# Attention into a mixture block on one core: q and k prepared for four heads at once, scores as three 64-row products, v loaded twice

## The chip, the cores and the metric

The kernel runs on one core of a Trainium2 chip. The metric is device time in microseconds (us), lower is better. Runs of the same kernel agree within about 0.3%.

The core has a matrix engine (TensorE, PE in the profile; its weight loads are PEld), three elementwise engines (VectorE, DVE; ScalarE, ACT; GpSimd, POOL), a queue engine (SyncE, SP), and 16 DMA engines that all queues share. On-chip memory has 128 partitions (rows). Matrix products land in PSUM, which here is used as banks of 128 x 512 float32.

## The reference

```python
q_n, k_n = rmsnorm(q, g_q), rmsnorm(k, g_k)        # q, k, v: 8 batches, 12 heads, 448 positions, 64 wide
scores = q_n @ k_n.T / sqrt(64)                    # per head, 448 x 448
attn = softmax(scores)                             # the sum gets 1e-9 added
x = (attn @ v), heads side by side                 # 8 x 448 x 768
xk = mu_k * x + (1 - mu_k) * x_prev                # x_prev: x one position earlier
xr = mu_r * x + (1 - mu_r) * x_prev
k = max(xk @ w_k, 0); v = k * k @ w_v              # 768 -> 1024 -> 768
out = sigmoid(xr @ w_r) * v
```

Everything is float32. The kernel multiplies in float16 and carries precision by splitting each operand into a rounded part ("hi") and the rest ("lo"); a product is then hi by hi, hi by lo and lo by hi.

## The kernel before, in words

**Three streams.** `attention()` (line 286) goes through 48 head pairs, six per batch. `weights()` (403) splits the weight matrices in 20 column tiles. `moe(b)` (418) does the three matrix products of a batch and writes the output. All three are Python generators. The loop at 551 takes one step at a time from the stream with the smallest planned time: an attention step advances its clock by 1/`ATT_STEPS` of a batch, so that `moe(b)` is written some 0.2 to 0.25 batches after the attention of batch b. The Tile framework then fixes each engine's order of instructions when the kernel is built, from this written order as priority and from when each instruction could be ready; `QK_PRIORITY` moves the score matmuls 400 places ahead. On the chip each engine follows its fixed order and waits on semaphores.

**One head pair.** Positions are spread so that position 7r + t of a head lies in row r, block t. A pair goes through these steps:

- `load` (139): q, k and v of two heads, each as 128 rows (head, r) of 7 x 64 columns, issued on ScalarE's queue, three or four pairs before that pair's scores.
- `stats` (148): squares of v (155) and of q and k (156) on ScalarE; POOL adds the halves of the squares (159) and multiplies k by the gains (160); VectorE sums (161, 162), scales (163 to 165), and takes 15 reciprocal roots at once by three Newton steps (`rsqrt`, lines 67 to 72). All these small numbers live in tile `ss`.
- `natural` (170): POOL multiplies q and k by their reciprocal norms (180), ScalarE rounds to `hi` (184), POOL subtracts (185), VectorE copies (186) so that `nat` holds 21 blocks of 64 rows x 128, hi and lo next to each other. Two DMA transposes on SyncE (189) make `stk`: for each head, 64 columns of hi stacked on 64 of lo, 128 rows. Then v: scale (191 to 193), hi (195), lo (196), a wrap-around copy (197), and four DMAs on SyncE (201, 202) that copy it on chip into `vv`, once as it is and once shifted by one block on the other 64 rows.
- `group_scores` (220) for groups of two, two, two and one block tiles: a tile of 128 x 448 scores is two matmuls over all 128 rows (234), four half-width ones for the seventh tile, which has one block of each head. Then the row maximum (237, DVE) and the exponential in place (238, ACT). A tile occupies one of four PSUM banks `sc`; in the first six pairs every third takes one of the two `mm` banks.
- `group_probs` (242): reciprocal of the sums (248, 249), hi of the probabilities (254, ACT), lo (255, DVE). Line 255 is the last reader of the bank, which is then free. DMA transposes on SyncE (257, 261) put the probabilities in `pT`.
- `attend` (266): 22 matmuls (273) in eleven passes, two heads each, half the array's columns per head; one pass has 64 rows only.

**Order of a pair's steps.** `attention()` runs the scores of group g + 1 before the probabilities of group g, and spreads `natural` of the next pair and `stats` of the one after over the four groups.

Of the kernel before, what the change touches and what calls it, by code (L numbers as in the profile page):

```python
# [7 lines left out]
F32 = mybir.dt.float32  # L8
# [16 lines left out]
QB = 2 * NT  # L25
# [9 lines left out]
ATT_STEPS = 132  # L35
# [23 lines left out]
def blocks(tile_, off, step):  # L59
    ap = tile_[:, :, :]  # L60
    return bass.AP(tensor=ap.tensor, offset=ap.offset + off, ap=[list(ap.ap[0]), [step, 2], [2 * HD, NT], [1, HD]])
# [13 lines left out]
def attn_moe_kernel(tc, q, k, v, g_q, g_k, mu_k, mu_r, w_k, w_v, w_r, out):  # L75
# [61 lines left out]
    LD, NAT, SUMS, PT, SC = {}, {}, {}, {}, {}  # L137

    def load(i):
        b, hp = pairs[i]  # L140
        pool, n = (pro[0], 1) if i < NP and i % 3 == 2 else (ap_, 2)
        qk = pool.tile([P, 2, S], F32, name="qk", bufs=n)
        vf = pool.tile([P, S], F32, name="vf", bufs=n)
        for dst, src in ((qk[:, 0, :], k), (qk[:, 1, :], q), (vf, v)):
            nc.scalar.dma_start(out=dst, in_=src[b, 2 * hp:2 * hp + 2].rearrange("h (p t) d -> (h p) (t d)", t=NT))
        LD[i] = qk, vf

    def stats(i):
        qk, vf = LD[i]
        qkv = qk.rearrange("p a (t d) -> p (a t) d", d=HD)  # L150
        xs = (pro[0] if i < NP else ap_).tile([P, 2 * NT, HD], F32, name="xn", bufs=1)
        ss = small.tile([P, 48], F32, name="ss", bufs=4)
        ST[i] = ss
        pt = ps.tile([P, 512], F32, name="tr", bufs=1)
        nc.scalar.activation(out=pt[:, 0:S], in_=vf, func=AF.Square, accum_out=ss[:, 45:46])
        nc.scalar.activation(out=xs, in_=qkv, func=AF.Square)
        nc.tensor.matmul(out=pt[:, 0:P], lhsT=ss[:, 45:46].bitcast(BF16)[:, 1:2].broadcast_to([P, P]), rhs=ident16, start=True, stop=True)
        yield
        nc.gpsimd.tensor_tensor(out=xs[:, :, 0:HD // 2], in0=xs[:, :, 0:HD // 2], in1=xs[:, :, HD // 2:], op=ALU.add)
        nc.gpsimd.tensor_tensor(out=qkv[:, 0:NT, :], in0=qkv[:, 0:NT, :], in1=bcast(G[:, :], NT), op=ALU.mult)  # L160
        nc.vector.tensor_reduce(out=ss[:, 0:14], in_=xs[:, :, 0:HD // 2], axis=AX.X, op=ALU.add)
        nc.vector.tensor_reduce(out=ss[:, 14:15], in_=pt[:, 0:P], axis=AX.X, op=ALU.max)
        nc.vector.tensor_scalar(out=ss[:, 7:14], in0=ss[:, 7:14], scalar1=gm[:, 3:4], scalar2=gm[:, 4:5], op0=ALU.mult, op1=ALU.add)
        nc.vector.tensor_scalar(out=ss[:, 0:7], in0=ss[:, 0:7], scalar1=1.0 / HD, scalar2=1e-6, op0=ALU.mult, op1=ALU.add)
        nc.vector.tensor_scalar(out=ss[:, 14:15], in0=ss[:, 14:15], scalar1=TINY, scalar2=2.0 ** -28, op0=ALU.max, op1=ALU.mult)
        yield
        rsqrt(nc, small, ss[:, 16:31], ss[:, 0:15], 15, "rs15")
        yield

    def natural(i):  # L170
# [4 lines left out]
        qk, vf = LD.pop(i)  # L175
        ss = ST.pop(i)
        qkv = qk.rearrange("p a (t d) -> p (a t) d", d=HD)
        sv = ss[:, 30:31]
        xn = ap_.tile([P, 2 * NT, HD], F32, name="xn", bufs=1)
        nc.gpsimd.tensor_tensor(out=xn, in0=qkv, in1=spread(ss[:, 16:30], HD), op=ALU.mult)  # L180
        nat = (pro[0] if i < NP and i % 2 else ap_).tile([P, 3 * NT, 2 * HD], F16, name="nat", bufs=1)
        hi, lo = blocks(nat, 0, QB * 2 * HD), blocks(nat, NT * 2 * HD, NT * 2 * HD + HD)
        xn4 = xn.rearrange("p (a t) d -> p a t d", a=2)
        nc.scalar.copy(out=hi, in_=xn4)  # L184
        nc.gpsimd.tensor_tensor(out=lo, in0=xn4, in1=hi, op=ALU.subtract)  # L185
        nc.vector.tensor_copy(out=nat[:, 0:QB, HD:], in_=nat[:, 0:QB, 0:HD])
        stk = ap_.tile([P, 2, 3 * NT, HD], F16, name="stk", bufs=2)
        for h in range(2):
            nc.sync.dma_start_transpose(out=stk[:, h], in_=nat[h * HD:(h + 1) * HD].rearrange("p a c -> p (a c)"))
        yield  # L190
        nc.vector.tensor_copy(out=st[:, hp:hp + 1], in_=sv)
        nc.vector.tensor_tensor(out=st[:, NP + hp:NP + hp + 1], in0=ss[:, 14:15], in1=sv, op=ALU.mult)  # L192
        nc.vector.tensor_scalar(out=ss[:, 46:47], in0=st[:, NP + hp:NP + hp + 1], scalar1=2.0 ** -15, scalar2=0.0, op0=ALU.mult, op1=ALU.add)
        vw = ap_.tile([P, 2, S + HD], F16, name="vw", bufs=1)
        nc.scalar.activation(out=vw[:, 0, 0:S], in_=vf, func=AF.Copy, scale=sv)
        nc.vector.scalar_tensor_tensor(out=vw[:, 1, 0:S], in0=vf, scalar=sv, in1=vw[:, 0, 0:S], op0=ALU.mult, op1=ALU.subtract)
        nc.vector.tensor_copy(out=vw[:, :, S:], in_=vw[:, :, 0:HD])
        vv = ap_.tile([P, 2, 2, S], F16, name="vv", bufs=2)
        for h in range(2):
            src = vw[h * HD:(h + 1) * HD]  # L200
            nc.sync.dma_start(out=vv[0:HD, h], in_=src[:, :, 0:S])
            nc.sync.dma_start(out=vv[HD:P, h], in_=src[:, :, HD:])
        NAT[i] = stk, vv, ss
        if hp == NP - 1:
            batch_scales(b)
        yield

    def batch_scales(b):
# [4 lines left out]
        nc.vector.tensor_scalar(out=sc[:, 2:4], in0=ismu, scalar1=sc[:, 0:1], scalar2=None, op0=ALU.mult)  # L213
# [6 lines left out]
    def group_scores(i, t0, n):  # L220
        stk, vv, ss = NAT[i]
# [3 lines left out]
        for t in range(t0, t0 + n):  # L225
            if i < PRO and (i * NT + t) % 3 == 2:
                sp = ps.tile([P, 512], F32, name="mm", bufs=MM_BUFS)
            else:
                sp = ps.tile([P, 512], F32, name="sc", bufs=4)
            for j in range(2):  # L230
                for h in (0, 1) if t == NT - 1 else (t % 2,):
                    q0, m, rows = (QB + t, 1, slice(h * HD, (h + 1) * HD)) if t == NT - 1 else (QB + t - h, 2, slice(0, P))
                    with tc.high_priority(offset=QK_PRIORITY):
                        nc.tensor.matmul(  # L234
                        out=sp[rows, 0:S], lhsT=stk[:, h, q0:q0 + m].rearrange("p t c -> p (t c)"),
                        rhs=stk[:, h, j * NT:(j + 1) * NT], start=(j == 0), stop=(j == 1))
# [29 lines left out]
    def attend(i):  # L266
        vv, ss = NAT[i][1:]
# [12 lines left out]
        nc.gpsimd.memset(x[:, 0, 0:1], 0.0)  # L280
        nc.gpsimd.tensor_copy(out=x[:, 0, 1:HD], in_=x[:, NT, 0:HD - 1])
        XT[pairs[i]] = x
        del NAT[i], SUMS[i]
        yield

    def attention():
        groups = [(i, t0, n) for i in range(len(pairs)) for t0, n in ((0, 2), (2, 2), (4, 2), (6, 1))]
        N = len(pairs)
        for i in range(3):
            load(i)  # L290
# [291 lines left out]
```

## Time and profile before

| What | Value |
|---|---|
| Time, median of three runs | 1256.08 us (1255.46 to 1259.13) |
| Span of the profiled execution, first to last instruction (its own time is not given otherwise) | 1253.7 us |
| PE, busy | 994.0 us |
| PEld, busy | 487.8 us |
| DVE, busy | 1019.3 us |
| ACT, busy | 776.9 us |
| POOL, busy | 700.0 us |
| DMA, mean | 155 GB/s |
| Mean granted TensorE clock | 0.929 |

How to read the profile: a row of the groups of instructions gives line, engine, operation, output<-inputs, shapes, count, then busy time in us, mean ns of one, and the idle time just before them with what ended it. A row of the busy times by stretch gives start:end, length, then busy us and count for each engine, the granted clock (1.00 is full), the DMA engines' mean busy share, and GB/s. A row of the timeline gives start in us, duration, engine, line, operation, tiles and shape, and how many were merged; a matmul's duration includes its way through the array, so the distance between starts is its price. A row of the waits reads: engine, line, who released it, us in total, times, longest.

### The profile page before, as it was taken

To read this page: it belongs to the slowest core of one execution; us is meant where nothing else is said; L and a number is where in the kernel's file an instruction comes from. 1 tells how busy PE (TensorE), PEld (TensorE's weight loads), DVE (VectorE), ACT (ScalarE), POOL (GpSimd) and SP (SyncE) were. 2 spreads that over 40 slices of the span, in tenths; PEclk is the share of its full clock that TensorE was granted. 3 is DMA by queue.
4 is the path that set the end of the run, shared out by engine and by line. 5 is a ranking of instruction groups with operands and counts; after the bars stand their busy time and mean duration, and the time that the engine had idled before them with its cause. 6 is when DMAs were issued, how large, how long until landed. Compare 5 with 4: busy or idle time off the path is not lost. (4 is left out here: it accounts for less than half of the span.)

```text
span 1253.7 us, 18496 instructions
## 1 busy us (share of the span) xinstructions
PE 994.0 (79%) x5551; PEld 487.8 (39%) x5551; DVE 1019.3 (81%) x2620; ACT 776.9 (62%) x1756; POOL 700.0 (56%) x702
## 2 busy tenths in 40 slices
PE   1344553766889888898988988989989989889998
PEld 0112221333444344344443444434434444445554
DVE  7989998889989897989778987998898979875200
ACT  3575655566667766677667766767667667755411
POOL 3614665545657664577457554865486557641821
PEclk9986666786999999998999999998999999999999
DMA  5899899889699899888997899988979999968001
GB/s 153 187 214 198 155 182 179 136 186 162 132 183 170 141 178 171 161 169 152 174 192 127 170 166 189 170 159 165 180 148 162 174 186 186 131 111 150 14 13 38
DMA packets 513188, 194.78 MB, mean 155 GB/s; under 512 B 449600, under 2 KB 509504, under 8 KB 513088
## 3 DMA queue, kind: packets, MB, share of 16 engines
q1 hardware_dynamic: 473248, 143.26, 68.2%
q10 hardware_dynamic: 39840, 50.35, 14.8%
q8 instruction: 43, 0.70, 0.2%
q14 instruction: 57, 0.47, 0.1%
HBM read 50.40 MB, written 11.01 MB: 49 GB/s over the span
## 5 line engine op out<-in xcount | busy, mean ns | idle before, releaser
L238 ACT ACTIVATE sc<-sc,sums 128x448 f32<-128x448 f32 x322 | 195.7, 608 | 127.3 <-DVE sums L237 125.5
L234 PE MATMUL sc<-stk 128*128 128x448 f16 (+1 forms) x736 | 191.1, 388 | 99.4 <-DVE ph L255 57.7
L255 DVE SCALAR_TENSOR_TENSOR ph<-sc,sums,ph 128x448 f16<-128x448 f32 x322 | 213.4, 675 | 56.0 <-ACT ph L254 55.6
L254 ACT ACTIVATE ph<-sc,sums 128x448 f16<-128x448 f32 x322 | 188.5, 636 | 93.3 <-DMA pT<-ph 51.3
L428 PE MATMUL mm<-wvh,kk 128*128 128x384 f16 x896 | 236.3, 332 | 4.2 <-DVE th L487 3.4
L428 PE MATMUL mm<-xk,wkh 128*128 128x448 f16 x768 | 220.1, 365 | 18.5 <-ACT kf L450 9.4
L237 DVE TENSOR_REDUCE sums<-sc 128x1 f32<-128x448 f32 x322 | 193.6, 613 | 14.1 <-PE sc L234 13.6
L273 PE MATMUL av<-pT,vv 128*64 128x448 f16 (+1 forms) x1056 | 164.3, 385 | 48.7 <-DMA pT<-ph 32.6
L428 PE MATMUL mm<-wrh,xr 128*128 128x384 f16 x672 | 179.8, 331 | 7.5 <-ACT th L484 2.9
L428 PEld LDWEIGHTS <-kk 128*128 128x128 f16 x1344 | 130.7, 99 | 102.7 <-issue 19.9
L428 PE MATMUL mm<-wvl,kk 128*128 128x384 f16 x448 | 148.4, 331 | 0.0
L428 PE MATMUL mm<-xk,wkl 128*128 128x448 f16 x384 | 139.6, 364 | 0.0
L180 POOL TENSOR_TENSOR xn<-qk,ss 128x896 f32<-128x896 f32 x48 | 82.1, 1711 | 98.0 <-DVE ss L72 50.0
L234 PEld LDWEIGHTS <-stk 128*128 128x128 f16 (+1 forms) x768 | 61.9, 106 | 187.7 <-issue 106.3
L428 PEld LDWEIGHTS <-xr 128*128 128x128 f16 x1008 | 97.2, 99 | 88.1 <-issue 23.5
L185 POOL TENSOR_TENSOR nat<-xn,nat 128x896 f16<-128x896 f32 x48 | 94.6, 1971 | 50.3 <-ACT nat L184 49.1
L273 PEld LDWEIGHTS <-vv 128*64 128x64 f16 (+1 forms) x1056 | 62.4, 114 | 149.4 <-issue 120.5
L428 PEld LDWEIGHTS <-wkh 128*128 128x128 f16 x768 | 75.7, 100 | 98.4 <-issue 33.2
L428 PE MATMUL mm<-wrl,xr 128*128 128x384 f16 x336 | 111.2, 331 | 0.0
L488 POOL TENSOR_TENSOR o<-th,bsc 128x384 f32<-128x384 f32 x48 | 43.4, 904 | 103.3 <-DVE th L487 52.3
L345 DVE SCALAR_TENSOR_TENSOR df<-x,bsc,df 128x448 f32<-128x448 f32 x90 | 83.1, 928 | 18.4 <-POOL df L344 18.3
L452 POOL TENSOR_TENSOR kf<-kf 128x448 f32<-128x448 f32 x64 | 62.9, 983 | 51.0 <-ACT kk L451 51.0
(124 smaller groups left out, 1743.0 us busy)
## 6 DMA issues: line engine op xcount, KB each, us to landing
vv<-vw SPq DMA_DIRECT2D x192, 112.0 KB, 3.3
qk<-in_k_dram ACTq DMA_DIRECT2D x48, 224.0 KB, 3.3
qk<-in_q_dram ACTq DMA_DIRECT2D x48, 224.0 KB, 4.1
vf<-in_v_dram ACTq DMA_DIRECT2D x48, 224.0 KB, 3.3
out_dram<-o SPq DMA_DIRECT2D x56, 192.0 KB, 3.5
raw<-in_moe_w_k_dram ACTq DMA_DIRECT2D x16, 384.0 KB, 4.7
raw<-in_moe_w_v_dram ACTq DMA_DIRECT2D x12, 512.0 KB, 4.0
raw<-in_moe_w_r_dram ACTq DMA_DIRECT2D x12, 384.0 KB, 4.9
```

Of the source, the lines that this page charges most:

```text
L180: nc.gpsimd.tensor_tensor(out=xn, in0=qkv, in1=spread(ss[:, 16:30], HD), op=ALU.mult)
L185: nc.gpsimd.tensor_tensor(out=lo, in0=xn4, in1=hi, op=ALU.subtract)
L234: nc.tensor.matmul(out=sp[rows, 0:S], lhsT=stk[:, h, q0:q0 + m].rearrange("p t c -> p (t c)"), rhs=stk[:, h, j * NT:(j + 1) * NT], start=( ...
L237: nc.vector.tensor_reduce(out=sums[:, t:t + 1], in_=sp[:, 0:S], axis=AX.X, op=ALU.max, negate=True)
L238: nc.scalar.activation(out=sp[:, 0:S], in_=sp[:, 0:S], func=AF.Exp, bias=sums[:, t:t + 1], accum_out=sums[:, 8 + t:9 + t])
L254: nc.scalar.activation(out=ph[:, j, 0:S], in_=sp[:, 0:S], func=AF.Copy, scale=r[:, j:j + 1])
L255: nc.vector.scalar_tensor_tensor(out=ph[:, j, S:], in0=sp[:, 0:S], scalar=r[:, j:j + 1], in1=ph[:, j, 0:S], op0=ALU.mult, op1=ALU.subtract)
L273: nc.tensor.matmul(out=av[h * HD:(h + 1) * HD, 0:S], lhsT=vv[0:kk, h, hl, slot * HD:(slot + 1) * HD], rhs=pT[0:kk, h, c, :], start=(j == 0 ...
L345: nc.vector.scalar_tensor_tensor(out=df, in0=xc, scalar=sc[:, MX + j:MX + j + 1], in1=df, op0=ALU.mult, op1=ALU.add)
L428: nc.tensor.matmul(out=ps_, lhsT=la(i, a), rhs=ra(i, c), start=(i == 0 and a + c == 0), stop=(i == n - 1 and a == 1))
L452: nc.gpsimd.tensor_tensor(out=kf, in0=kf, in1=kf, op=ALU.mult)
L488: nc.gpsimd.tensor_tensor(out=o[:, hs].rearrange("p (c n) -> p c n", n=P), in0=th.rearrange("p (c n) -> p c n", n=P), in1=spread(rsu[:, ND ...
```

## The change

- **Quads.** q and k are prepared for four heads (two pairs) at once by `prep(u)`: tiles of 128 rows (two halves of two heads) x 896, loaded by four DMAs on ScalarE's queue; one `rsqrt` on 28 columns for both pairs. `load(u + 2)` stands at the end of quad u, and `prep(u + 1)` is spread over quad u's eight groups, k first and then q, through one `nat` buffer.
- **Scores.** `nat` now holds hi and lo of two heads side by side, 14 blocks, without the extra copy; a transposed tile has head 0 on rows 0 to 63 and head 1 on rows 64 to 127. A tile of scores is three products (hi hi, hi lo, lo hi) over 64 rows. In a two-tile group each head has its own bank; in the group of one both heads share a bank.
- **v.** `vload` brings v from memory twice, on 64 rows each, the second time shifted by one block, by three DMAs on SyncE into one buffer `vf`; `vprep` takes the square (of one copy), a power-of-two scale by integer shifts instead of a reciprocal root, hi, and lo in two instructions for the four blocks that need it. No copy on chip.
- **Planning.** `ATT_STEPS` is 126 instead of 132, as a batch of attention has 120 steps instead of 126.

```diff
+    def load(u):
+        b, j = quads[u]
+        LD[u] = []
+        for n, src in enumerate((k, q)):
+            pool, nb = (pro[0], 1) if u == 1 else (ap_, QK_BUFS)
+            t = pool.tile([P, 2, S], F32, name="qk" if pool is ap_ else "qk%d" % n, bufs=nb)
+            for x in range(2):
+                h0 = 4 * j + 2 * x
+                nc.scalar.dma_start(out=t[x * HD:(x + 1) * HD], in_=src[b, h0:h0 + 2].rearrange("h (r t) d -> r h (t d)", t=NT))
+            LD[u].append(t)
+
+    def vload(i):
...
+        vf = ap_.tile([P, 2, S], F32, name="vf", bufs=1)
+        src = v[b, 2 * hp:2 * hp + 2].rearrange("h (r t) d -> r h (t d)", t=NT)
+        nc.sync.dma_start(out=vf[0:HD], in_=src)
+        nc.sync.dma_start(out=vf[HD:P, :, 0:S - HD], in_=src[:, :, HD:S])
+        nc.sync.dma_start(out=vf[HD:P, :, S - HD:S], in_=src[:, :, 0:HD])
...
+    def prep(u):
+        ss = small.tile([P, 2 * NSS], F32, name="ss", bufs=2)
+        for n, t in enumerate(LD[u]):
+            tv = t.rearrange("p h (t d) -> p (h t) d", d=HD)
+            xs = ap_.tile([P, 2 * NT, HD], F32, name="xs", bufs=1)
+            nc.scalar.activation(out=xs, in_=tv, func=AF.Square)
+            nc.gpsimd.tensor_tensor(out=xs[:, :, 0:HD // 2], in0=xs[:, :, 0:HD // 2], in1=xs[:, :, HD // 2:], op=ALU.add)
+            if n == 0:
+                nc.gpsimd.tensor_tensor(out=tv, in0=tv, in1=bcast(G[:, :], 2 * NT), op=ALU.mult)
+            nc.vector.tensor_reduce(out=ss[:, 2 * NT * n:2 * NT * (n + 1)], in_=xs[:, :, 0:HD // 2], axis=AX.X, op=ALU.add)
+            yield
...
+        rsqrt(nc, small, ss[:, NSS:2 * NSS], ss[:, 0:NSS], NSS, "rs28")
+        yield
+        T = [ap_.tile([P, 2, 2 * NT, HD], F16, name="stk", bufs=3) for x in range(2)]
+        for n, t in enumerate(LD.pop(u)):
...
+            nat = pool.tile([P, 2 * NT, P], F16, name="nat", bufs=1)
+            hi, lo = heads(nat, 0), heads(nat, NT * P)
+            t4 = t.rearrange("p h (t d) -> p h t d", d=HD)
+            nc.scalar.copy(out=hi, in_=t4)
+            yield
+            nc.gpsimd.tensor_tensor(out=lo, in0=t4, in1=hi, op=ALU.subtract)
+            for x in range(2):
+                nc.sync.dma_start_transpose(out=T[x][:, n], in_=nat[x * HD:(x + 1) * HD].rearrange("p a c -> p (a c)"))
+            yield
...
+    def vprep(i):
...
+        nc.scalar.activation(out=vh[0:HD].rearrange("p h t d -> p h (t d)").bitcast(BF16), in_=vf[0:HD], func=AF.Square, accum_out=vs[0:HD, 0:1])
+        nc.tensor.matmul(out=pt[:, 0:HD], lhsT=vs[0:HD, 0:1].bitcast(BF16)[:, 1:2].broadcast_to([HD, P]), rhs=ident16[0:HD, 0:HD], start=True, stop=True)
+        yield
+        nc.vector.tensor_reduce(out=vs[:, 1:2], in_=pt[:, 0:HD], axis=AX.X, op=ALU.max)
...
+        nc.scalar.activation(out=vh.rearrange("p h t d -> p (h t d)"), in_=vf.rearrange("p h s -> p (h s)"), func=AF.Copy, scale=sv)
+        yield
...
         for h in range(2):
...
+            nc.vector.scalar_tensor_tensor(out=vl[:, h], in0=vf4[:, h, 0::2, :], scalar=sv, in1=vh[:, h, 0::2, :], op0=ALU.mult, op1=ALU.subtract)
...
     def group_scores(i, t0, n):
...
+        banks = []
+        for j in range(n):
+            tag, nb = ("mm", MM_BUFS) if i < PRO and (i * NT + t0 + j) % 3 == 2 else ("sc", 4)
+            banks.append(ps.tile([P, 512], F32, name=tag, bufs=nb))
+        with tc.high_priority(offset=QK_PRIORITY):
+            for m, (kl, ql) in enumerate(((0, 0), (0, 1), (1, 0))):
+                for h in range(2):
+                    hs = slice(h * HD, (h + 1) * HD)
+                    nc.tensor.matmul(
+                        out=banks[h][:, 0:S] if n == 2 else banks[0][hs, 0:S],
+                        lhsT=T[hs, 1, ql * NT + t0:ql * NT + t0 + n].rearrange("p t c -> p (t c)"),
+                        rhs=T[hs, 0, kl * NT:(kl + 1) * NT].rearrange("p t c -> p (t c)"),
+                        start=(m == 0), stop=(m == 2))
+        for j, sp in enumerate(banks):
...
     def attention():
...
         for gi, (i, t0, n) in enumerate(groups):
+            u, x = divmod(i, 2)
             if t0 == 0:
+                vp = vprep(i + 1) if i + 1 < N else iter(())
+                if not x and u + 1 < NQ:
+                    pre = prep(u + 1)
+            next(pre, None)
+            yield
+            if t0:
+                next(vp, None)
                 yield
...
             if t0 == 6:
...
+                if i + 2 < N:
+                    vload(i + 2)
+                if x and u + 2 < NQ:
+                    load(u + 2)
```

The lines of `stats`, `natural` and the old `load`, `group_scores` and `attention` that these replace can be read in the listing above. What the passes of `attend` do stays the same; they read `vh` and `vl` instead of `vv`.

More of the change, by code (lines that the diff above doesn't have):

```diff
@@ L24 @@
 NH = D_MODEL // 2
-QB = 2 * NT
+QK_BUFS = 3
 TINY = 2.0 ** -60
@@ L56, in spread, with heads @@
     return bass.AP(tensor=ap.tensor, offset=ap.offset, ap=[list(x) for x in ap.ap] + [[0, n]])
-def blocks(tile_, off, step):
+def heads(tile_, off):
     ap = tile_[:, :, :]
-    return bass.AP(tensor=ap.tensor, offset=ap.offset + off, ap=[list(ap.ap[0]), [step, 2], [2 * HD, NT], [1, HD]])
+    return bass.AP(tensor=ap.tensor, offset=ap.offset + off, ap=[list(ap.ap[0]), [HD, 2], [2 * HD, NT], [1, HD]])
 def rsqrt(nc, pool, y, a, n, tag):
@@ L136, in attn_moe_kernel @@
     pairs = [(b, hp) for b in range(B) for hp in range(NP)]
-    LD, NAT, SUMS, PT, SC = {}, {}, {}, {}, {}
-    def load(i):
-        b, hp = pairs[i]
[L141 to L157, printed above, removed]
-        yield
[L159 to L168, printed above, removed]
@@ L170, in natural @@
-    def natural(i):
+    quads = [(b, j) for b in range(B) for j in range(NP // 2)]
+    LD, VF, VV, TQ, SUMS, PT, SC = {}, {}, {}, {}, {}, {}, {}
+    NSS = 4 * NT
+    def load(u):
[8 more added lines that the diff above has]
+            LD[u].append(t)
@@ L174, in natural @@
         st = BS[b]
[L175 to L182, printed above, removed]
@@ L192, in natural @@
[L192 to L196, printed above, removed]
@@ L197, in natural @@
[L197 to L203, printed above, removed]
+        vf = VF.pop(i)
+        vh = ap_.tile([P, 2, NT, HD], F16, name="vh", bufs=2)
+        vl = ap_.tile([P, 2, 4, HD], F16, name="vl", bufs=2)
@@ L220, in group_scores @@
     def group_scores(i, t0, n):
-        stk, vv, ss = NAT[i]
+        T = TQ[i]
         if t0 == 0:
@@ L224, in group_scores @@
         sums = SUMS[i]
[L225 to L236, printed above, removed]
+        banks = []
[12 more added lines that the diff above has]
+        for j, sp in enumerate(banks):
+            t = t0 + j
             nc.vector.tensor_reduce(out=sums[:, t:t + 1], in_=sp[:, 0:S], axis=AX.X, op=ALU.max, negate=True)
@@ L274, in attend @@
                     out=av[h * HD:(h + 1) * HD, 0:S],
-                    lhsT=vv[0:kk, h, hl, slot * HD:(slot + 1) * HD],
+                    lhsT=vl[0:kk, h, slot // 2, :] if hl else vh[0:kk, h, slot, :],
                     rhs=pT[0:kk, h, c, :],
```

60 lines of the change are left out of this document (30 added, 30 removed).

## The prediction, made before the result

> **What bounds the kernel now.** I read the page, then the busy times by stretch, the waits inside the long middle, and the order of TensorE's work there.
>
> ```profile
> span 1253.7 us, 18496 instructions
> ...
> PE 994.0 (79%) x5551; PEld 487.8 (39%) x5551; DVE 1019.3 (81%) x2620; ACT 776.9 (62%) x1756; POOL 700.0 (56%) x702
> ```
>
> ```profile
> 0.00:373.00 373.00, 208.11 (x1032) 96.53 (x1032) 335.52 (x889) 220.24 (x467) 191.14 (x174) 0.82 0.87 173
> 400.00:1100.00 700.00, 618.73 (x3538) 302.28 (x3537) 604.79 (x1555) 478.39 (x1101) 432.09 (x440) 0.97 0.92 166
> 1162.00:1254.00 92.00, 85.85 (x505) 49.16 (x504) 12.69 (x16) 20.81 (x48) 36.32 (x40) 1.00 0.09 22
> ```
>
> The columns are PE, weight loads, DVE, ACT and POOL busy, granted clock, DMA share and GB/s. Three stages: a front (two batches of attention and the weights, DVE busy 335.52 of 373), a middle, and a tail of 92 us in which TensorE alone works. In the middle three things are nearly full: PE 88%, DVE 86%, DMA 0.92.
>
> The second table is the same view for the instructions that touch tile `ss` (statistics of q, k, v).
>
> ```profile
> 0.00:1254.00 1254.00, 11.30 (x48) 4.94 (x48) 328.54 (x960) 62.47 (x96) 82.15 (x48) 0.93 0.83 155
> 0.00:373.00 373.00, 4.04 (x15) 1.72 (x15) 100.85 (x283) 16.20 (x25) 24.41 (x14) 0.82 0.87 173
> 400.00:1100.00 700.00, 6.82 (x31) 3.03 (x31) 214.04 (x638) 41.13 (x63) 54.37 (x32) 0.97 0.92 166
> ```
>
> POOL's x32 is one multiplication per head pair: the middle does 32 pairs, 21.9 us each. Per pair PE is busy 19.3 us, DVE 18.9, ACT 14.9, POOL 13.5, and PE is idle 2.5.
>
> **The change: VectorE.** Twenty of its instructions per pair touch `ss`, 328.54 us in all; the change redoes them and drops two copies (L186, L197).
>
> ```profile
> L186 DVE COPY nat<-nat 128x896 f16<-128x896 f16 x48 | 32.4, 675 | 9.0 <-POOL nat L185 5.8 <-POOL x L280 3.1
> ...
> L161 DVE TENSOR_REDUCE ss<-xn 128x14 f32<-128x448 f32 x48 | 29.1, 607 | 4.4 <-POOL xn L159 4.0 <-ACT x L279 0.3
> ...
> L163 DVE TENSOR_SCALAR ss<-ss,gm 128x7 f32<-128x7 f32 x48 | 26.7, 557 | 0.4
> ...
> L197 DVE COPY vw<-vw 128x128 f16<-128x128 f16 x48 | 24.8, 518 | 0.2
> ...
> L67 DVE TENSOR_SCALAR ss<-ss 128x15 int32<-128x15 int32 x48 | 15.3, 319 | 0.3
> ...
> L391 DVE TENSOR_SCALAR WSC<-WSC 128x1 int32<-128x1 int32 x20 | 2.8, 139 | 0.0
> ```
>
> ```profile
> L196 DVE SCALAR_TENSOR_TENSOR vw<-vf,ss,vw 128x448 f16<-128x448 f32 x48 | 45.6, 951 | 10.3 <-ACT vw L195 9.9
> ```
>
> The next row is all that touches tile `rs`: the nine Newton steps, L70 to L72.
>
> ```profile
> 0.00:1254.00 1254.00, 128.90 (x441) 0.93 0.83 155
> ```
>
> Removed: 328.5 + 32.4 + 24.8 = 386 us. Added: the Newton steps and the two shifts before them (L67, and L68 priced like it) run once per two pairs on 28 columns instead of 15: (128.9 + 2 x 15.3) / 2 = 80, and 3 for the longer rows. The sums of squares (L161) keep their count and size: 29. The two scalings, priced like L163, are half as many pairs' worth: 24 x 2 x 0.557 = 27. For v, per pair: one reduction and three one-column steps, each at most twice L391's 0.139, so 4 x 0.14 to 0.28, take 0.16: 48 x 0.64 = 31. The low part of v is now two instructions of 256 columns each: between 256/448 of L196 (0.54) and L196 whole (0.95); it is nearer to the first, but has a start of its own, so 0.68: 96 x 0.68 = 65. Sum 235, saving about 150 us (120 to 170): DVE falls from 18.9 to 15.8 us per pair.
>
> **The change: DMA.**
>
> ```profile
> q1 hardware_dynamic: 473248, 143.26, 68.2%
> q10 hardware_dynamic: 39840, 50.35, 14.8%
> ...
> vv<-vw SPq DMA_DIRECT2D x192, 112.0 KB, 3.3
> ```
>
> SyncE's queue (q1) loses the four copies of v per pair, 22.0 MB; at q10's 14.8% for 50.35 MB that is 6.5 points. The q/k transposes shrink from 21 to 14 blocks of 64 per head row, a third of their 48 x 2 x 64 x 21 x 128 x 2 bytes = 33.0 MB; what is left of q1 after v and the output (11.0 MB) is 58.5 points for 110 MB, so 5.8 points go. Loading v twice, in float32, adds 11.0 MB and 3.2 points. DMA falls by about 9 of 83 points, in the middle from 0.92 to 0.82.
>
> Queues: SyncE issues ten DMAs per pair where it issued eleven, since v's three loads come to it from ScalarE's queue. They wait for the last reader of the only `vf` buffer (DVE's low part); behind them stand the probabilities' transposes, for which PE's `av` waits. That reader is ahead of those probabilities in DVE's own order, so I cost it at nothing. The loads of q and k are now issued just ahead of their use, where they were one or two pairs ahead, and ScalarE's second rounding of a quad waits for the transposes of the first, with the exponentials queued behind it. Uncovered, that is 24 waits of up to 3.3 us, the landing time in the `vv` row; ACT has 21.9 - 14.9 = 7 us per pair free, so nothing.
>
> **ScalarE and POOL.**
>
> ```profile
> L156 ACT ACTIVATE xn<-qk 128x896 f32<-128x896 f32 x48 | 45.8, 954 | 11.6 <-POOL x L280 3.7 <-POOL nat L185 2.9 <-DVE ss L161 2.6
> ...
> L195 ACT ACTIVATE vw<-vf,ss 128x448 f16<-128x448 f32 x48 | 32.3, 673 | 17.1 <-DMA vv<-vw 14.7 <-DVE ss L72 1.8 <-issue 0.4
> ...
> L155 ACT ACTIVATE tr<-vf 128x448 f32<-128x448 f32 x48 | 26.4, 549 | 9.7 <-DMA qk<-in_q_dram 6.6 <-DVE rs L70 0.9 <-DVE ss L162 0.8
> ```
>
> v lies on 64 rows (twice), so its square and its rounding go from 448 to 896 columns; from L155 to L156 that costs 0.40 us, twice per pair: ACT 14.9 to 15.7, beside other work. POOL's element counts stay the same.
>
> **TensorE, which decides.**
>
> ```profile
> 861.95 0.54 PE L234 MATMUL sc<-stk 128*128 128x448 f16 x2
> ...
> 864.60 0.54 PE L234 MATMUL sc<-stk 128*128 128x448 f16 x2
> ...
> 865.55 0.55 PE L234 MATMUL sc<-stk 128*128 128x448 f16 x2
> ...
> 868.43 0.57 PE L234 MATMUL sc<-stk 128*64 128x448 f16 x4
> ...
> 869.49 0.55 PE L234 MATMUL sc<-stk 128*128 128x448 f16 x2
> ...
> 874.36 0.92 PE L234 MATMUL sc<-stk 128*128 128x448 f16 x4
> 875.11 0.33 PE L428 MATMUL mm<-wrh,xr 128*128 128x384 f16 x1
> ...
> 879.39 0.54 PE L234 MATMUL sc<-stk 128*128 128x448 f16 x2
> ```
>
> ```profile
> 1159.08 0.33 PE L428 MATMUL mm<-wrl,xr 128*128 128x384 f16 x1
> 1159.24 0.33 PE L428 MATMUL mm<-wrh,xr 128*128 128x384 f16 x1
> 1159.50 2.51 PE L273 MATMUL av<-pT,vv 128*64 128x448 f16 x21
> 1161.93 0.34 PE L428 MATMUL mm<-wvh,kk 128*128 128x384 f16 x1
> ```
>
> Four score matmuls in a row take 875.11 - 874.36 = 0.75 us, so a slot of 448 columns is 0.187 us. Side by side does work: 21 half-width `av` matmuls need 2.43 us, not 21 x 0.187 = 3.9. But from 1159.24 to 1161.93 go 2.69 us, and one 384-column slot (0.16) with eleven of 448 (ten pairs and one alone, 2.06) is 2.22. The other 0.47 pays four changes of array shape: into half width, to 64 rows (one pass has 64 rows), back, and out; a visit, in and out, costs 0.24. The Trainium skill (TensorEngine Tiling (Array Packing), Tiling Modes, Key Properties) says that a change of tiling mode drains TensorE; by it every visit is charged, by a bound of nothing for the new shape none is, and the trace sides with the rule.
>
> Scores per pair now take 14 slots and one visit: six tiles of two matmuls in the full shape, and the seventh with four half-width ones in two slots. After, a two-tile group is three products for each of two heads on 64 rows: three slots if the heads run side by side, six if not.
>
> Will they? Each head writes its own PSUM bank, and a bank is free only when VectorE has made the low part of the probabilities that lie in it.
>
> ```profile
> PE sc L234 <- DVE ph L255: 28.0, 21, 4.7
> ```
>
> ```profile
> L255 DVE SCALAR_TENSOR_TENSOR ph<-sc,sums,ph 128x448 f16<-128x448 f32 x322 | 213.4, 675 | 56.0 <-ACT ph L254 55.6
> ```
>
> That wait is PE's longest in the middle, and two banks of a group come free at least 0.68 us apart, while one head's three products take 0.56. In the quoted stretch the seventh tile is at 868.43. Before it, tiles 4 and 5 start at 864.60 and 865.55, with other matmuls between; after it come tile 0 at 869.49, tiles 1 and 2 together at 874.36, tile 3 at 879.39. So no group has its two tiles next to each other, although scores have priority. The order within TensorE is fixed when the kernel is built, from readiness, so I expect the first head's three products to be placed when its bank comes free and the second's later: six slots and two visits.
>
> So split, a pair has 3 x 6 + 3 = 21 slots: 7 x 0.187 = 1.3 us more, and up to six visits more; one is shared where tiles of two groups adjoin, as at 874.36, so 5 x 0.24 = 1.2. PE goes from 19.3 to 21.8 us busy per pair (20.6 if the visits were free), in a period of 21.9.
>
> **The sum.** Middle: DVE and DMA have room, PE has none. The busy sum counts ends that overlap (a 384-column matmul is shown with 0.33, the next starts 0.16 later), so a period of 21.6 is possible: 0.3 us on the 36 pairs between 373 and 1162, 11 us less. Front: DVE's share of 150 us is (100.85 / 328.54), 46 us, less some 7 for a first chain that prepares four heads before any score; the half that is not chain or DMA is taken, 16 to 20, take 16. Tail: unchanged. 1253.7 - 11 - 16 = 1226.7. The profiled execution shows only its span; the median of the three runs is 2.4 above it, so 1229.
>
> **Rivals.** *Side by side holds* (banks come free together, for instance because q's transposes come last and find all four banks empty). Then 3 x 3 + 3 = 12 slots and four visits: 2 x 0.187 less, 3 x 0.24 more, PE 19.7. With DVE at 15.8 and DMA 11% lower, I give the pair 19.7 to 20.6: 47 to 79 us, and 25 in the front: 1152 to 1184, take 1165. For it: `av` is nearly always paired; against: its heads share a bank.
>
> *TensorE over its limit* (slower). Split as above, but the 2.5 us that PE idles per pair are latency of transposes and chains, and stay in part. From 21.9 on, each us per pair costs 36. With 1.0 to 1.8 of the 2.5 left, less 0.2 for overlapping ends, the pair takes 22.6 to 23.4: +25 to +54, with 16 off in front, 1265 to 1294, take 1280. For it: the longest wait after the banks' is for transposes, which remain. Against: in the tail PE is busy 85.85 of 92 us, so it can run full.
>
> *The seventh tile serializes*: its two heads lie on different rows but in one bank. If they took turns, that is three slots, 0.56 us a pair, 20 us on the forecast: 1249. The Trainium skill (same page, Restrictions and Gotchas, PSUM Pressure) says that different row tiles cannot access one bank at the same time. No run so far shows such a pair.
>
> **Chances.** Split, as forecast: 0.52, its own range 1205 to 1257. Side by side 0.25, over the limit 0.17, one bank 0.06. The range goes a little below the second case and leaves out the upper three fifths of the third (0.10): 1148 to 1276. A measurement of this kernel can tell 0.3%, 4 us. Faster: 0.25 + 0.38 of the first + 0.02 = 0.65; same 0.11 of the first + 0.02 = 0.13; slower 0.22.
>
> **What would show it.** DVE near 870 us busy; DMA share in the middle near 0.82; score matmuls in TensorE's order as three of one head, others, three of the other, 0.187 apart; a gap of about 0.1 more at each change of shape; PE above 95% busy in the middle. I am wrong if the two heads' products start within a few ns of each other, if PE stays below 90%, or if ScalarE waits for q, k or v more than a few us per pair.

## The result, and the profile after

The changed kernel takes 1270.91 us (median of four runs, 1268.06 to 1274.97) where the kernel before takes 1255.77 in the same comparison: a ratio of 1.0136, 95% interval 1.0101 to 1.0172. It is slower, by about 15 us. The forecast of 1229 had the sign wrong; the time lies in its range. Single runs of one kernel lie up to 0.8% apart in this comparison (1249.25 to 1259.13 for the kernel before), more than the 0.3% given at the start, so a few us between two kernels are read as no difference below.

The head of the page, the queues, and busy times by stretch (columns as before):

```profile
span 1266.3 us, 18774 instructions
...
PE 1061.6 (84%) x5935; PEld 488.2 (39%) x5935; DVE 905.6 (72%) x2212; ACT 808.8 (64%) x1756; POOL 679.9 (54%) x678
...
q1 hardware_dynamic: 423328, 132.24, 58.6%
q10 hardware_dynamic: 32928, 39.34, 12.9%
```

```profile
0.00:373.00 373.00, 216.49 (x1060) 92.03 (x1060) 317.77 (x795) 229.64 (x467) 198.64 (x174) 0.81 0.80 159
400.00:1100.00 700.00, 660.80 (x3773) 297.39 (x3775) 529.37 (x1298) 507.18 (x1124) 396.90 (x412) 0.98 0.80 147
```

VectorE lost 114 us of busy time, the DMA engines 9.6 points of SyncE's queue, and their share in the middle went from 0.92 to 0.80. Two engines got fuller there: TensorE, 660.80 of 700 us, 94%, where it was 88%, and ScalarE, 507.18 us where it was 478.39.

The last row of the group of attention outputs (`x<-av`) ends the attention. It stands at 1162.05 in the kernel before:

```profile
1162.05 0.63 ACT L279 ACTIVATE x<-av,ss 128x448 f32<-128x448 f32 x1 [1.50 <-PE av L273]
```

and in the kernel after, followed by the busy times of what remains behind it:

```profile
1135.24 0.63 ACT L295 ACTIVATE x<-av,bstat 128x448 f32<-128x448 f32 x1 [4.39 <-PE av L289]
```

```profile
1135.00:1267.00 132.00, 123.82 (x739) 71.83 (x735) 17.71 (x24) 30.01 (x73) 49.39 (x55) 0.99 0.08 22
```

These three rows hold the whole result. The attention ends 27 us *earlier*, 1135.2 instead of 1162.05. But where 92 us with 505 matmuls used to remain, 131 us with 739 now do: 39 us more. 39 - 27 = 12 is the 12.6 us by which the span grew. Which matmuls come last is decided when the kernel is built: in TensorE's fixed order 504 matmuls of the second part (lines 428 and 448) stand behind the last attention matmul before, 735 after.

Why so much is left over, TensorE's timeline shows. The rows give start, duration, tile and count; in this stretch products of one head and products of two heads at once stand between other matmuls:

```profile
809.20 0.74 PE L246 MATMUL sc<-stk 64*128 64x448 f16 x3
809.87 0.50 PE L448 MATMUL mm<-wvh,kk 128*128 128x384 f16 x2
...
814.27 0.75 PE L246 MATMUL sc<-stk 64*128 64x448 f16 x6
...
817.33 0.74 PE L246 MATMUL sc<-stk 64*128 64x448 f16 x3
818.00 0.50 PE L448 MATMUL mm<-wvh,kk 128*128 128x384 f16 x2
```

Three products of one head alone take 0.74 us; all six, side by side, 0.75. Of the runs of score products in TensorE's order 151 are of three. Of the 432 places where a product of a two-tile group could start beside one of the other head, 90 are used, about a fifth. Not all of these are one group's two heads: counted from the seventh tile at 807.75, the six at 814.27 are the second head of one group and the first head of the next. So the two heads of a group mostly stand apart, the split that was forecast.

TensorE's records can be added up further. From each start to the next I take a slot (0.187 us for 448 columns, 0.1625 for 384, nothing for the second of two that start together), an excess under 0.2 us where the array's shape changes, and excesses of 0.2 us and more, which are waits. Over the profiled execution, in us (the kernels below the second row come from the experiments):

| Kernel | slots | changes of shape | waits | of these after 200 us | last attention output | behind it | span |
|---|---|---|---|---|---|---|---|
| before | 844 | 37 | 295 | 167 | 1162 | 92 | 1253.7 |
| after | 892 | 68 | 236 | 102 | 1135 | 131 | 1266.3 |
| v part alone | 842 | 41 | 255 | 126 | 1124 | 87 | 1211.0 |
| v part, extra slots | 907 | 45 | 220 | 100 | 1124 | 115 | 1239.0 |
| after, two products | 838 | 69 | 245 | 99 | 1130 | 88 | 1217.8 |
| after, VectorE's work back | 892 | 69 | 235 | 102 | 1161 | 107 | 1267.7 |
| after, in step | 846 | 67 | 281 | 138 | 1175 | 91 | 1266.0 |
| v part, five banks | 845 | 39 | 247 | 114 | 1094 | 103 | 1196.9 |

The change adds 48 us of slots and 31 of shape changes, 79 in all, and gets 59 of waits back (and 7 in small gaps): 13 us longer. This is an account of where the time went; that the added work is the cause, the experiments have to show.

### The profile page after: what moved, and what is told of

It reads as the page before. It is cut to its first block, busy times and chain, and to the rows that moved or that the text cites. A ratio compares the mean times of both kernels' runs of the same rounds, so it can differ in the third digit from the quotient of the medians.

```text
span 1266.3 us, 18774 instructions
## 1 busy us (share of the span) xinstructions
PE 1061.6 (84%) x5935; PEld 488.2 (39%) x5935; DVE 905.6 (72%) x2212; ACT 808.8 (64%) x1756; POOL 679.9 (54%) x678
## 5 line engine op out<-in xcount | busy, mean ns | idle before, releaser
L246 PE MATMUL sc<-stk 64*128 64x448 f16 (+1 forms) x1104 | 228.9, 372 | 63.2 <-DVE ph L271 48.0
L448 PEld LDWEIGHTS <-kk 128*128 128x128 f16 x1344 | 126.4, 99 | 113.9 <-issue 39.8
L289 PE MATMUL av<-pT,vh 128*64 128x448 f16 x672 | 143.0, 386 | 22.3 <-DMA pT<-ph 9.2
L246 PEld LDWEIGHTS <-stk 64*128 64x128 f16 (+1 forms) x1152 | 71.9, 100 | 196.2 <-issue 136.9
L186 POOL TENSOR_TENSOR nat<-qk,nat 128x896 f16<-128x896 f32 x48 | 92.2, 1921 | 63.2 <-ACT nat L184 63.1
L167 POOL TENSOR_TENSOR xs<-xs 128x448 f32<-128x448 f32 x48 | 55.1, 1148 | 127.3 <-ACT xs L166 126.9
L264 DVE TENSOR_SCALAR sums<-sums 128x2 f32<-128x2 f32 x192 | 71.6, 374 | 71.9 <-ACT sc L254 70.7
L448 PEld LDWEIGHTS <-wkh 128*128 128x128 f16 x768 | 72.5, 100 | 95.4 <-issue 41.9
L179 POOL TENSOR_TENSOR qk<-qk,ss 128x896 f32<-128x896 f32 x48 | 82.3, 1735 | 46.0 <-DVE ss L72 32.6
L166 ACT ACTIVATE xs<-qk 128x896 f32<-128x896 f32 x48 | 45.6, 950 | 85.6 <-DMA qk<-in_q_dram 43.8
```

Of the source, the lines that this page charges most:

```text
L179: nc.gpsimd.tensor_tensor(out=tv, in0=tv, in1=spread(ss[:, NSS + 2 * NT * n:NSS + 2 * NT * (n + 1)], HD), op=ALU.mult)
L186: nc.gpsimd.tensor_tensor(out=lo, in0=t4, in1=hi, op=ALU.subtract)
L246: nc.tensor.matmul(out=banks[h][:, 0:S] if n == 2 else banks[0][hs, 0:S], lhsT=T[hs, 1, ql * NT + t0:ql * NT + t0 + n].rearrange("p t c -> ...
L264: nc.vector.tensor_scalar(out=r, in0=sums[:, 8 + t0:8 + t0 + n], scalar1=1e-9, scalar2=2.0 ** -15, op0=ALU.add, op1=ALU.mult)
L289: nc.tensor.matmul(out=av[h * HD:(h + 1) * HD, 0:S], lhsT=vl[0:kk, h, slot // 2, :] if hl else vh[0:kk, h, slot, :], rhs=pT[0:kk, h, c, :] ...
L448: nc.tensor.matmul(out=ps_, lhsT=la(i, a), rhs=ra(i, c), start=(i == 0 and a + c == 0), stop=(i == n - 1 and a == 1))
```

## The experiments

The theory at the outset: TensorE's own sum decides, because heads' products stand alone. First rival: the first scores, which come at 59.9 us instead of 37.1, pass their lateness on to the end. Second rival: ScalarE's new waits for q and k (79.6 us in all). Ratios are to the kernel before, with their 95% intervals.

**Two banks in one tile.** To make both heads' banks come free together:

```diff
-        banks = []
-        for j in range(n):
-            tag, nb = ("mm", MM_BUFS) if i < PRO and (i * NT + t0 + j) % 3 == 2 else ("sc", 4)
-            banks.append(ps.tile([P, 512], F32, name=tag, bufs=nb))
+        two = ps.tile([P, 2, 512], F32, name="sc", bufs=2)
+        banks = [two[:, j, :] for j in range(n)]
```

> The changed kernel, with both heads of a group in one tile of two PSUM banks (two such tiles instead of four single banks), so that both banks come free together and the six products can stand side by side. Theory (TensorE's own sum decides, and the change's products stand alone): the changed kernel spends 892 us on matmul slots and 68 us on changes of shape, the kernel before 844 and 37. Paired, a head pair needs 12 slots instead of about 19.4, so 66 us of slots and some 20 us of shape changes go; some waits grow because the banks are handed out in twos. 1190 to 1230 us. Rival 1 (the later first scores, 59.9 us instead of 37.1, pass through to the end and the pairing matters little): 1250 to 1275. Rival 2 (ScalarE's new waits for q and k hold attention): 1250 to 1275.

Its control has the same tiles, but one head's products before the other's:

```diff
-            for m, (kl, ql) in enumerate(((0, 0), (0, 1), (1, 0))):
-                for h in range(2):
+            for h in range(2):
+                for m, (kl, ql) in enumerate(((0, 0), (0, 1), (1, 0))):
```

> As e1_two_bank, in the same tiles and the same places, but the three products of head 0 come first and then the three of head 1, so that none can stand side by side except at the seam. The difference to e1_two_bank is the price of side by side alone. Theory: 3 more slots in each of 144 two-tile groups and in the group of one, 3 x 0.187 x 192 = 108 us of TensorE more than e1_two_bank; the time 60 to 110 us above it, 1260 to 1320. Rivals 1 and 2: within 20 us of e1_two_bank.

Measured: 1434.67 us, 1.1443 (1.1411 to 1.1475), and 1436.71, 1.1452 (1.1433 to 1.1471). Both expectations missed. Banks handed out by twos starve everything: in the first, TensorE is busy for 550.69 of the middle's 700 us and VectorE for 450.31. And the control is none: in its trace, too, all 432 products of the two-tile groups that could start beside one of the other head do so (within 0.04 us), as here, although the code names one head's three first:

```profile
701.15 0.75 PE L244 MATMUL sc<-stk 64*128 64x448 f16 x6
```

So the two runs do the same work in the same time, and what side by side is worth they don't show. They do show that the products pair by themselves where both outputs come free together.

**The v part alone**, on the kernel before: `vload` and `vprep` of the change take the place of v's lines in `load`, `stats` and `natural`; q, k and scores stay. The stream has more steps, hence the other pace.

```diff
-ATT_STEPS = 132
+ATT_STEPS = 151
...
-                    lhsT=vv[0:kk, h, hl, slot * HD:(slot + 1) * HD],
+                    lhsT=vl[0:kk, h, slot // 2, :] if hl else vh[0:kk, h, slot, :],
```

> The kernel before with the change's v part alone (v loaded twice, power-of-two scale, no copy on chip); q, k and the scores as before. TensorE's work is that of the kernel before. Theory: DVE loses about 60 us and the DMA engines 60 us of work while TensorE gains none, so it is faster than before: 1225 to 1245 us. Rival 2 in another form (the single v buffer and its loads on SyncE's queue hold attention): 1256 to 1285.

Measured: 1218.88 us, 0.9713 (0.9679 to 0.9746): faster than both kernels, by more than expected. The change is thus two changes: the v part takes some 36 us off, and the q, k and score part puts 52 on.

**Two products instead of three**, on the kernel after: the product of k's low part with q's high part is left out, so the scores lose precision.

```diff
-            for m, (kl, ql) in enumerate(((0, 0), (0, 1), (1, 0))):
+            for m, (kl, ql) in enumerate(((0, 0), (0, 1))):
...
-                        start=(m == 0), stop=(m == 2))
+                        start=(m == 0), stop=(m == 1))
```

> The changed kernel without the third product of the scores (lo of k by hi of q is left out), so 12 instead of 18 matmuls in the two-tile groups of a pair and 4 instead of 6 in the last; nothing else changes. Theory: some 6.5 slots of 0.187 us fewer per pair, 58 us in all, and the time falls by 40 to 60 us: 1210 to 1230. Rivals 1 and 2: less than 15 us.

Measured: 1220.89 us, 0.9717 (0.9672 to 0.9763), 50 less than after, as expected. Loads, first scores and VectorE's work are those of the kernel after. 54 us of slots are gone, and 43 of the 131 us behind the last attention output.

**The first scores.** The weights' stream begins later, to leave the engines to the first quad:

```diff
-        Stream([(0.0, lambda: wgen)], 0.0, W_RATE / (3 * NA + 1)),
+        Stream([(0.0, lambda: wgen)], 0.09, W_RATE / (3 * NA + 1)),
```

> The kernel after, with the stream of weight tiles begun later (0.09 instead of 0.0 of a batch), so that the attention prologue has the engines for itself. If TensorE's own sum decides (the theory), the first scores come some 10 us earlier and the end moves by less than 8 us: 1262 to 1278. If the later first scores (59.9 us instead of 37.1) pass through to the end (first rival), the end moves by about what the first scores do: 1250 to 1262. If ScalarE's waits for q and k decide (second rival), no change.

Measured: 1286.71 us, 1.0259 (1.0221 to 1.0298). The edit missed its aim: the first score product stays at 59.9 us, so the weights were not what held it, and weights that come later cost 16 us. It does not test the first rival.

**The loads.** k of the quad after next is issued earlier, and q after the second pair's first group:

```diff
+            if t0 == 2 and u + 2 < NQ:
+                load(u + 2, (x,))
...
-                if x and u + 2 < NQ:
-                    load(u + 2)
```

> The kernel after, with the load of k two quads ahead issued after the first pair's first group and that of q after the second pair's, not both behind the second pair's last; the same buffers. If TensorE's sum decides, 1264 to 1276. If ScalarE's waits for the loads (44 us in all) decide (second rival), half of them or more come off the end: 1240 to 1256. If the first scores decide (first rival), no change.

Measured: 1272.43 us, 1.016 (1.0127 to 1.0193), no change. But the waits did not change either (46.7 and 32.8 us, where they were 43.8 and 35.8): this too missed its aim.

**TensorE's work added to a kernel that has neither rival.** The v part alone, each first score product done twice, the second overwriting the first:

```diff
-            for j in range(2):
+            for r, j in enumerate((0, 0, 1)):
...
-                        rhs=stk[:, h, j * NT:(j + 1) * NT], start=(j == 0), stop=(j == 1))
+                        rhs=stk[:, h, j * NT:(j + 1) * NT], start=(r < 2), stop=(r != 1))
```

> The kernel before with the v part alone, and every first score product done twice (the second overwrites the first): 7 slots of 0.187 us more a pair, 63 us of TensorE in all, no change of array shape, no other work. If TensorE's sum decides here too, 0.65 to 0.8 of it comes through, as of the 79 us that the change adds: 1260 to 1269 beside 1218.9 without. If the loss of the changed kernel came from the first scores or the loads, this kernel has neither and stays at 1217 to 1232.

Measured: 1241.42 us, 0.9917 (0.9889 to 0.9946). 22.5 us of the 63 come through (28 between the two profiled executions), less than expected, more than the rivals allow. The table shows the rest: the attention ends at 1124 as without, 26 us of waits after 200 us are filled, and what finds no room stands behind the last attention output: 115 us instead of 87. Here, work added to TensorE does not lengthen the attention; it pushes the mixture block's matmuls back.

**Part of VectorE's saving put back.** The kernel after, with 126 copies that nobody needs:

```diff
+            if u >= 3:
...
+                for h in (0, 1, 0):
+                    nc.vector.tensor_copy(out=dv, in_=nat[:, :, h * HD:(h + 1) * HD])
```

> The kernel after, with 126 copies of 896 columns added on VectorE (about 85 us, what q and k for four heads and the missing stack copy saved it beside the kernel with the v part alone). If TensorE's sum decides, VectorE's saving buys little: 1268 to 1285. If the bank ring (four score banks, each kept from its first product until its low part is made) decides the pace, VectorE's queue is part of the ring and most of a quarter or more of the 85 us comes through: 1290 to 1320.

Measured: 1272.93 us, 1.0154 (1.0101 to 1.0207), as expected: nothing. The copies take 66.9 us instead of 85, and VectorE's busy time goes from 905.6 to 964.0 us, half of what the change saved. The copies' row in the groups, and the last attention output in this kernel:

```profile
L190 DVE COPY dv<-nat 128x896 f16<-128x896 f16 x126 | 66.9, 531 | 4.0 <-POOL nat L186 2.2 <-POOL x L300 1.3
```

```profile
1160.81 0.63 ACT L299 ACTIVATE x<-av,bstat 128x448 f32<-128x448 f32 x1 [7.27 <-PE av L293]
```

The attention ends 25.6 us later (1160.81 against 1135.24), and the kernel ends at the same time. The run with the shared bank (below) does the same in another way: its last attention output comes at 1148.53, 13 us later, and its span is 1267.4. So the pace of the attention does not set the end of the kernel after, and what acts through that pace alone, as ScalarE's waits for q and k do, does not either. That goes against the second rival, and against the first as far as late scores mean a late attention.

**Products in step.** To get the pairs without tiles of two banks, each of a group's six products is placed behind the one before, second head first:

```diff
-                for h in range(2):
+                for h in (1, 0):
...
+                    if prev is not None:
+                        tc.add_manual_dep(getattr(mmi, "ins", mmi), getattr(prev, "ins", prev).name, mybir.DependencyInfo(mybir.DependencyClass.NoSync, mybir.DependencyReason.DATA), reason="pair")
+                    prev = mmi
```

> The kernel after with one more rule of order on TensorE: the six products of a two-tile group stand in the order second head, first head, and so on, each behind the one before; banks as they are. If TensorE's sum decides, groups come to 3 to 4 slots instead of 6, some 7 of 21 slots (1.3 us) a pair less, and the time falls as it did without the third product, to 1205 to 1235. If the first scores or the loads decide, 1262 to 1276. If waiting for the second bank starves the probabilities as it did with tiles of two banks, above 1290.

Measured: 1264.75 us, 1.0091 (1.0052 to 1.013). A miss: 6 us under the kernel after instead of 36 or more, and the two intervals overlap. The edit does what it should: 330 of the 432 places side by side are used, where the kernel after uses 90. In the timeline a first product stands alone and the other five take 0.74 us, as three did:

```profile
671.51 0.36 PE L247 MATMUL sc<-stk 64*128 64x448 f16 x1
671.80 0.38 PE L293 MATMUL av<-pT,vh 128*64 128x448 f16 x1
...
672.12 0.74 PE L247 MATMUL sc<-stk 64*128 64x448 f16 x5
```

TensorE has 47 us less to do, 46 of them slots. But its waits rise by 45. The score group's row in the kernel after, and the same row here (idle time before, and who ended it, stand last):

```profile
L246 PE MATMUL sc<-stk 64*128 64x448 f16 (+1 forms) x1104 | 228.9, 372 | 63.2 <-DVE ph L271 48.0
```

```profile
L247 PE MATMUL sc<-stk 64*128 64x448 f16 (+1 forms) x1104 | 189.6, 379 | 82.3 <-DVE ph L275 68.1 <-DMA stk<-nat 12.9 <-DVE WIN L417 0.8
```

The last attention output comes at 1175, and 91 us follow. So here, it seems, the attention sets the end, as in the kernel before. Its pace is that of the four banks, which go round as a ring: from the end of a tile's low part to the row maximum of the tile four places later, and from there to the end of that tile's low part, are on average 4.53 + 8.22 us in the middle of the kernel before, 4.41 + 7.94 after, and 6.17 + 6.73 in step. A product that waits for the second head's bank leaves the first head's empty meanwhile.

**Five banks.** The small products (v's bound, the column maxima) move to the bank of the attention output, and the scores get a fifth:

```diff
-        pt = ps.tile([P, 512], F32, name="tr", bufs=1)
+        pt = ps.tile([P, 512], F32, name="av", bufs=1)
...
-            tag, nb = ("mm", MM_BUFS) if i < PRO and (i * NT + t0 + j) % 3 == 2 else ("sc", 4)
+            tag, nb = ("mm", MM_BUFS) if i < PRO and (i * NT + t0 + j) % 3 == 2 else ("sc", 5)
```

> The kernel after with five score banks instead of four (the small products of v's bound and the column maxima share the bank of the attention output). If TensorE's sum decides (its waits after 200 us are down to 102 us, no less than in any kernel so far), the fifth bank brings little: 1255 to 1275. If the ring of banks decides, the ring gets a quarter longer: 1215 to 1245.

> The kernel with the products of a group in step, and five score banks. In step with four banks TensorE had 47 us less to do than in the kernel after and waited 45 us more, and the ring of banks went from 12.35 to 12.90 us. If it was the ring that took the gain back, a fifth bank returns most of it: 1215 to 1240. If pairing brings nothing for another reason, 1255 to 1270.

> The kernel before with the v part alone, and five score banks. TensorE waits 126 us after 200 us there, 25 more than the least seen. If a fifth bank takes them, 1190 to 1212; if the ring is not what holds it, 1212 to 1225; if the shared bank costs more than it brings, above 1225.

Measured: on the kernel after 1301.95 us, 1.0377 (1.032 to 1.0434); in step 1311.31, 1.0451 (1.0406 to 1.0495); on the v part alone 1199.46, 0.9565 (0.9519 to 0.9611). The last is as expected, the other two are misses on the wrong side. With the fifth bank the wait goes one stage on: ScalarE, waits in the middle of the kernel after,

```profile
ACT sc L254 <- DVE sums L253: 69.0, 70, 3.3
ACT xs L166 <- DMA qk<-in_q_dram: 26.3, 11, 5.5
```

and with five banks,

```profile
ACT sc L254 <- DVE sums L253: 57.3, 49, 3.2
ACT ph L270 <- DMA pT<-ph: 56.0, 42, 3.5
```

where the second row has grown from 5.2 us: the two buffers of probabilities wait for their transposes.

**A third such buffer** (`PH_BUFS = 3`; on the kernel after and its version in step with `X_BUFS = 6`, for room):

> The kernel before with the v part alone, five score banks and three buffers of probabilities instead of two. ScalarE waited 38.6 us there for the transposes that free them. If that holds the pace, 1180 to 1196; if TensorE's sum decides by now (1199.5 with 105 us of it after the last attention output), 1194 to 1206.

> The kernel after with five score banks, three buffers of probabilities, and six instead of seven of the attention outputs (for room). If the two buffers were what took the fifth bank back (79.6 us of waits), 1250 to 1275, and no less, since TensorE's sum decides there; if the shared bank was, 1290 to 1310 as without.

> The same with the products of a group in step. If the two buffers took the gain (100.5 us of waits), TensorE's 47 us come out at last: 1210 to 1245. If the shared bank or the wait for the second bank did, 1265 to 1312.

Measured: 1193.08 us, 0.9496 (0.9458 to 0.9535), on the v part, 6 us less than with two buffers, though the intervals overlap; 1310.59, 1.0461 (1.0399 to 1.0523), on the kernel after, a miss; 1283.14, 1.0218 (1.0158 to 1.0277), in step, 28 less than with two buffers but still above the version with four banks.

**The shared bank by itself** (the first half of the five banks' edit, on the kernel after), and a fifth bank that shares another (in step):

```diff
-        pt = ps.tile([P, 512], F32, name="tr", bufs=1)
+        pt = ps.tile([P, 512], F32, name="mm", bufs=MM_BUFS)
```

> The kernel after with the small products (v's bound, the column maxima) in the bank of the attention output, and four score banks as before: the shared bank by itself. If sharing is what costs the versions with five banks, 1290 to 1310; if the fifth bank itself, 1262 to 1280.

> The kernel with the products of a group in step and five score banks, the small products sharing the two banks of the second part's matmuls instead of that of the attention output. If sharing the attention output's bank cost it, 1225 to 1262; if the fifth bank itself does, 1280 to 1312, as with the other shared bank.

Measured: 1270.39 us, 1.0125 (1.0089 to 1.016): sharing the bank costs nothing. 1334.23, 1.0632 (1.0578 to 1.0685): the fifth bank costs as much or more with the other bank shared. So it is the fifth bank itself that harms the kernels that prepare four heads at once, while the v part gains 19 us by it.

Why stays open, but the traces narrow it. On the kernel after, the fifth bank does not quicken the ring: a tile takes 3.1 us with four banks and with five, as each tile is now held for 10.6 us, not 7.9, from its row maximum to the end of its low part (on the v part it goes from 3.05 to 2.97). TensorE's waits after 200 us rise by 20 us, small gaps between matmuls by another 20, at a mean granted clock of 0.902 instead of 0.933. The last attention output comes at 1167.90, 33 us later, and yet the second part has not used the time: 774 of its matmuls, 138 us, stand behind it, more than in the kernel after. In both in-step versions with five banks and two buffers it is the same 774. So in these kernels TensorE waits while work for it stands further back in its fixed order.

The old stacked scores fed from four heads prepared at once would split the q, k part further; that was not tried.

The version with the v part alone, five banks and three buffers, at 1193.08 us, beats both kernels.

## Why the prediction was wrong

*VectorE* was right in direction and too large: the change saves 114 us of busy time, and 150 (120 to 170) were forecast. Counted row by row, as the forecast did, the removed rows hold 401 us and the added 239, 162 less. Of the 48 us between, 14 are other rows that became longer, and 34 are overlap: all rows together add up to 1185.8 us before and 1037.8 after, where VectorE is busy for 1019.3 and 905.6. That this saving would bring time was wrong: half of it, put back, costs nothing.

*DMA* was right: 0.80 in the middle (forecast 0.82). ScalarE's load, 0.7 us a pair more (808.8 against 776.9 over 48 pairs), was forecast at 0.8. Its waits for q and k, taken at nothing, are 79.6 us; what they cost at the end no run measured alone, and the run with the copies speaks against a cost.

*TensorE* was right in mechanism and too dear in size. The split came as forecast, with the two heads' products three and three and a price at each change of shape. Forecast were 2.5 us a pair, 120 in all; measured are 79, since about a fifth of the products run side by side after all (48 us of slots, forecast 1.3 x 48 = 62) and visits adjoin more often (31 us of shape changes, forecast 58). Forecast was TensorE above 95% busy in the middle; it is 94%.

*The sum* failed at its last term. "11 us less" in the middle and 16 in front would put the last attention output 27 us earlier, from 1162 to 1135. It comes at 1135.24, but by luck, as two misses of 25 us cancel. The last attention output of batch 1 ends the front. Before and after:

```profile
373.25 0.63 ACT L279 ACTIVATE x<-av,ss 128x448 f32<-128x448 f32 x1
```

```profile
382.45 0.63 ACT L295 ACTIVATE x<-av,bstat 128x448 f32<-128x448 f32 x1 [0.86 <-PE sc L246]
```

It is 9 us later, not 16 earlier: the first scores come 23 us later, where the forecast took 7 for the first chain. The 36 pairs behind it go at 20.9 us each, where it was 21.9 before and 21.6 was forecast: 36 us less, not 11. **The failed step is "Tail: unchanged".** It holds TensorE's 2.5 us against one pair's period, as if filling the attention's idle time were free. That idle time was where the matmuls of the second part went. Its work is the same, and with 79 us more for the scores and 59 us of waits given back, the rest stands at the end: 131 us instead of 92. That the kernel after is held by TensorE's work is shown by the run with two products (54 us of slots less, 50 us of time), by the copies and the shared bank (attention later, end unmoved), and by the extra slots in the other direction. One reading covers these runs: the end is the later of two bounds, the attention's pace plus some 90 us, and TensorE's whole sum plus the waits that nothing fills; in the kernel before and in step the first one would decide, in the kernel after the second. That reading is argued, not shown, and the kernels with four heads at once and five banks don't fit it: they end later than either bound.

*The rivals.* "TensorE over its limit" gave 1280 (1265 to 1294) at 0.17, and the time fits; its mechanism did not happen, since it put the loss in the pair's period, 22.6 to 23.4 us, and that fell to 20.9. "Side by side holds" was made to happen in step: slots fell by 46 us, but the banks took the gain. "The seventh tile serializes" did not happen (below).

What the runs leave open: how much would come off the end if the first scores came 23 us sooner, since the edit meant for it left them where they were. TensorE's records suggest little: its waits up to 200 us are 128 before and 134 after. Open as well is whether another planned pace (`ATT_STEPS`, and the lag of the second part) would put more of its matmuls into the waits; on the kernel after, neither was varied.

## What to carry to other kernels

Where an engine serves two streams and one of them has priority, count its work for both: here, what the first stream added beside idle time was paid by the second, at the end, and the pace of the first showed nothing of it. Side by side, too, has to be planned for: where both outputs came free together all products paired, where one bank came free well before the other most pairs fell apart, and forcing them together cost in empty banks what it saved in slots. And a change of two parts should be run as two: the half that only saves (v, and then the bank and the buffer that it leaves to be the next wait) gave 5%, and the other half had hidden it.

## What the runs showed of the hardware

Two heads that lie on different rows of the array and write different rows of *one* bank do run side by side. A seventh tile of the kernel after (64 x 64 tiles, three products of two heads):

```profile
850.70 0.76 PE L246 MATMUL sc<-stk 64*64 64x448 f16 x6 [0.31 <-DVE ph L271]
```

Six products take 0.76 us, where three alone take 0.74; 135 of 144 such pairs in this kernel start within 0.05 us of each other. The rule that the prediction weighed (the Trainium skill, TensorEngine Tiling (Array Packing), Restrictions and Gotchas, PSUM Pressure: different row tiles cannot access one bank at the same time) would make that six slots in a row, 3 x 0.187 us more, 1.3 us. Here the measurement decides: they can, for two tiles that write separate rows.

A change of array shape costs 0.10 us on average, counted as for the table (28.8 us for 281 of them in the middle before, 53.0 for 539 after), a little under the 0.12 that half a visit was taken at.
